# A recurrence with four experts behind it: three weight loads moved, four copies given to VectorE, VectorE's stated order changed

## The chip, the cores and the metric

The kernel runs on one core of one Trainium2 chip. A core has TensorE (PE) for matrix products, with a part of its own for loading the stationary operand (PEld in the profile), VectorE (DVE), ScalarE (ACT), GpSimd (POOL), and SyncE (SP), which here issues nearly all transfers (DMAs). Products land in PSUM, all else lives in SBUF. The metric is device time in microseconds (us), as the median of several runs; times inside an execution come from one profiled execution, counted from its first instruction.

## The reference

Two blocks follow each other, all in float32. The first is a recurrence over 768 tokens for 4 batches and 8 heads of width 40 (`[4, 8, 768, 40]` for each of r, k, v, w, a, b), with a state of 40x40 for each batch and head:

```python
for t in range(S):
    y[:, :, t] = np.einsum('bhd,bhde->bhe', rt, state)
    Sa = np.einsum('bhde,bhe->bhd', state, at)
    state_decay = state * wt[:, :, None, :] - np.einsum('bhd,bhe->bhde', Sa, bt)
    state = state_decay + np.einsum('bhd,bhe->bhde', vt, kt)
```

Its output becomes x of 3072 tokens by 320. The second block mixes four experts for each token:

```python
p = domain_probs / (domain_probs.sum(-1, keepdims=True) + 1e-09)
for e in range(E):                      # E = 4, F = 1024
    h = np.maximum(x @ w1[e], 0.0)
    out += p[:, e:e + 1] * (h @ w2[e])
```

## The kernel before

**Units and steps.** The tokens of a batch are cut into 12 chunks of 64. A unit is one chunk of two batches, so there are 24 units; unit u has chunk u // 2. For each unit, `within` does the work that needs no state: the running product of w (`G`, by two transposes and a scan on VectorE), its inverse (`gp`), the transposed operands A, V and R (`AT`, `VT`, `RT`), and the products between tokens of the chunk (`pfe` and `pe`, copied as `F` and `ET`; `pc`, copied as `VC`; `pev`, copied as `EV`). `substitute` solves the triangular system of the chunk: VectorE makes `M` from blocks of `F` (L599 to L615), and then a chain of small operations on `Z` runs on GpSimd (L620 to L639). `merge` makes `Qc`, `QTc` and `QT` of it. `step` is the part with the state: `prn` (state times A, and the turned state), `RH` = `prn` + `EV` on VectorE (L700), then ScalarE copies `SN`, then `psat`, `pxr`, `SX` (VectorE, L441), `pdy`, the new state (L773, L774) and the output `Y`, which transfers from SBUF to SBUF place as x transposed (`xT`, L793).

**Where V and R are turned.** For units 0 to 2 the natural V and R are turned by TensorE (`pVT`, `pRT`, L112) and ScalarE copies each out of PSUM in three copies: one of 128 rows, two of 64 rows that also swap halves (L472, L474). From unit 3 on VectorE turns them by itself from `rawV` and `rawR` (L282), which come in by 16 small transfers a unit (`load_raw`), placed in SP's queue by `later` and `begin_later`, three or six at a time between pieces of the experts' work.

**The experts.** w1 is read anew for each chunk in pieces: piece k holds half of the columns of one expert, 512 KB and two of 64 KB (L341), into one of two `w1p` buffers, or for some early pieces into a `sums` buffer. `used(n)` issues the next piece once piece n's products stand in the program; the transfer itself waits until TensorE is done with the buffer. `up_last` does 16 products of 64x64 with a piece (`ph`, small), `up_main` 16 of 128x128, and ScalarE writes relu of them as `hs` (L827). For chunks from the second on the down product of two units is done in seven block products instead of eight: VectorE adds weights (`sum_w`, L915) and halves of `hs` (`a`, named sum_a, L950), TensorE makes `p`, and VectorE adds `p` by the gate into the output tile (`osb`, named out, L842). Three PSUM buffers are shared by `ph` and `p` (tag "mm"), five by the recurrence (tag "big").

**What sets the order.** TensorE runs in the order in which the program is written, which mixes pieces of the experts' work (`mix`, `gap`) between the parts of the recurrence. VectorE's order is written out by hand in `VECTOR_ORDER` for what stands in it (units 1 to 7 and the additions up to out23); each name is tied behind the one before it at the end of the kernel. Later instructions of VectorE are placed by a scheduler. In it stand, for the change: `VC2.0 blocks2.0 blocks2.1 ET2.0 M2`; `G5.0 sum_w1 ... gll5 RH3.0 RH3.1`; `G6.0 ... gll6 sum_w5 RH4.0 RH4.1`. SP works its queue in program order where `keep_in_program_order` says so, as for every piece.

The loop over units, u = 1 to 23, runs steps 1 to 23; while step u runs, unit u + 1 is merged, unit u + 2 is solved, and the loads of unit u + 3 are issued. In the profile step 2 begins (`prn`) at 109.69 us, step 3 at 143.39, step 4 at 175.92, step 5 at 218.15 and step 6 at 249.63.

Of the kernel before, what the change touches and what calls it, by code (L numbers as in the profile page):

```python
# [9 lines left out]
ALU = mybir.AluOpType  # L10
ACTF = mybir.ActivationFunctionType
AX = mybir.AxisListType
BEHIND = mybir.DependencyInfo(mybir.DependencyClass.NoSync, mybir.DependencyReason.DATA)


VECTOR_ORDER = """
    Qc1 QTc1 G2.0 G2.1 gl2 G02 scan2 gll2 out1 gp2 1/gp2 N2 K2 AT2 AG2 VC2.0 blocks2.0 blocks2.1 ET2.0 M2 M02 Z12
    Z22 ET2.1 VC2.1 out2 G3.0 G3.1 gl3 G03 scan3 SX1.1 gll3 SX1.0 VT3 RT3 AT3 AG3 Y1.1 Y1.0 S+1.0 S+1.1 SG1.0 SG1.1
    gp3 1/gp3 N3 K3 out3 VC3.0 VC3.1 Qc2 QTc2 RH2.0 RH2.1 G4.0 G4.1 gl4 G04 blocks3.0 blocks3.1 M3 M03 Z13 Z23 ET3.0
    ET3.1 out4 scan4 gll4 AT4 AG4 SX2.0 SX2.1 VT4 RT4 Y2.1 Y2.0 S+2.0 YG2 SG2.0 S+2.1 gp4 SG2.1 1/gp4 N4 K4 out5  # L20
    VC4.1 VC4.0 sum_w0 Qc3 QTc3 ET4.0 blocks4.0 blocks4.1 ET4.1 M4 M04 Z14 Z24 G5.0 sum_w1 G5.1 gl5 G05 scan5 gll5
    RH3.0 RH3.1 sum_w2 AT5 AG5 out6 SX3.0 SX3.1 sum_w3 VT5 Y3.1 Y3.0 S+3.0 YG3 SG3.0 S+3.1 gp5 SG3.1 1/gp5 RT5 N5 K5
    sum_w4 out7 VC5.1 VC5.0 Qc4 QTc4 ET5.0 blocks5.0 blocks5.1 ET5.1 M5 M05 Z15 Z25 G6.0 G6.1 gl6 G06 scan6 sum_a4
    gll6 sum_w5 RH4.0 RH4.1 sum_w6 AT6 AG6 sum_a0 sum_a1 sum_a2 sum_a3 SX4.0 SX4.1 sum_w7 VT6 sum_w8 Y4.1 Y4.0 S+4.0
    YG4 SG4.0 S+4.1 gp6 SG4.1 1/gp6 RT6 N6 K6 out8 out9 out10 out11 sum_a5 VC6.1 VC6.0 Qc5 QTc5 ET6.0 blocks6.0
    blocks6.1 ET6.1 out12 out13 M6 M06 Z16 Z26 out14 out15 sum_w9 sum_a6 G7.0 G7.1 gl7 G07 RH5.0 RH5.1 scan7 gll7
    sum_a7 sum_a8 sum_a9 AT7 AG7 out16 out17 out18 out19 sum_w10 sum_w11 SX5.0 SX5.1 sum_w12 sum_w13 sum_w14 sum_a10
    sum_a11 out20 sum_a12 out21 sum_a13 VT7 out22 sum_a14 out23
"""


# [1 line left out]
def kernel(  # L33
# [38 lines left out]
    nc = tc.nc  # L72

    B, H, S, D = r.shape
# [12 lines left out]
    names, made, stated_order = VECTOR_ORDER.split(), {}, []  # L87
# [30 lines left out]
    def big(name):  # L118
# [6 lines left out]
        out=ident[:], in_=ident[:], pattern=[[1, P]], compare_op=ALU.is_equal, fill=0.0,  # L125
# [5 lines left out]
    for t, n, op in ((upf, L, ALU.is_gt), (diagf, Q, ALU.is_equal)):  # L131
        nc.vector.memset(t[:], 1.0)
        for q in range(P // n):
            o = slice(q * n, (q + 1) * n)
            nc.gpsimd.affine_select(
                out=t[o], in_=t[o], pattern=[[1, n]], compare_op=op, fill=0.0, base=0, channel_multiplier=-1,
# [153 lines left out]
    ins = nc.vector.transpose(out=unit_cols[:], in_=dealt(diagf[:, None, :].to_broadcast([P, H, Q])))  # L290
# [31 lines left out]
    def load_piece():  # L322

        k = len(pieces)
        e, x = k // 2 % E, k % 2
        if k in in_sums:
            t = sums[in_sums[k]]
        else:
            t = sb.tile([P, PIECE], FP32, name="w1p", tag="w1p", bufs=2)
        q = Piece()  # L330
        q.main = t[:, 0:2 * HF * P].rearrange("p (g c) -> p g c", g=2)
        q.last = t[:, 2 * HF * P:PIECE].rearrange("p (f c) -> p f c", c=P)
        cols = slice(x * HF * P, (x + 1) * HF * P)
        moves = [(q.main, moe_w1[e, 0:2 * P, cols].rearrange("(g p) c -> p g c", p=P))]
        for i in range(2):
            half_cols = slice((2 * x + i) * HF // 2 * P, (2 * x + i + 1) * HF // 2 * P)
            moves.append(
                (q.last[i * DT:(i + 1) * DT], moe_w1[e, 2 * P:DM, half_cols].rearrange("d (f c) -> d f c", c=P))
            )
        for to, src in moves:  # L340
            tc.keep_in_program_order(nc.sync.dma_start(out=to, in_=src))  # L341
        pieces.append(q)

    def used(n):
# [30 lines left out]
    def half(s):  # L375
        return slice(64 * s, 64 * s + 64)
# [66 lines left out]
    def within(q):  # L443

        n = q.n
# [12 lines left out]
        ins = nc.vector.tensor_tensor(out=q.gl[:], in0=G[:, L::L][:, :, None], in1=first[:, :, 0:1], op=ALU.mult)  # L458
# [4 lines left out]
        def turn_rv():  # L463
            VT = sb.tile([P, 2 * NJ, L], FP32, name="VT", tag="turned", bufs=3)
            q.RT = sb.tile([P, 2 * NJ, L], FP32, name="RT", tag="RT", bufs=2)
            for x, t in (("V", VT), ("R", q.RT)):
                if q.u >= PADDED:
                    noted(turn_raw(t[:], n["raw" + x][:]), x + "T", q.u)
                    continue
                p = turn(f"p{x}T", tok(n["padded" + x]), q.u == 1)[:].rearrange("p (j i t) -> p j i t", i=2, t=L)  # L470
                to = t[:].rearrange("p (i j) t -> p j i t", i=2)
                nc.scalar.copy(out=to[:, 0::2], in_=p[:, 0::2])  # L472
                for r in range(2):
                    nc.scalar.copy(out=to[half(r), 1::2], in_=p[half(1 - r), 1::2])  # L474
            return VT

        if q.u == 1:
# [66 lines left out]
        p = banks("pfe")  # L544
# [494 lines left out]
    def run(gen, n=99):  # L1039
        if gen is None:  # L1040
            return
        for _ in range(n):
            if next(gen, gen) is gen:
                break
# [111 lines left out]
    for u in range(1, NU):  # L1156
        in_order[0] = True
        q = units[u]
        m = s_next = w = w_next = iter(())
        if u + 1 < NU:  # L1160
            m, s_next = merge(units[u + 1]), begin_step(u + 1)
            w_next = ws[u + 1]
        if u + 2 < NU:
            w = ws[u + 2]

        def gap(n, pieces=None):
            here[0] = at = 4 * u + n
            run(sum_ops, sums_at.get(at, 0))
            mix((1 if at in sparse else 2) if pieces is None else pieces)

        early = u < EARLY
        if early:
            begin_later(len(later))
        ahead = u + 3 < NU and u in range(EARLY, EARLY + 3)
        if ahead:
            go(load_raw(begin(u + 3), "W"))
        if early:
            lead()
        if u == 1:
            run(s, 1)  # L1180
            run(w_next)
        else:
            run(w_next, 99 if early else 1)
            run(s, 1)
        gap(0)


        if early:
            run(s, 1)
        run(w, 1)  # L1190
        if not early:
            run(w_next)
            run(s)

        if early:
            run(w, 1)
            gap(1, 2 if u + 1 == EARLY else None)
            run(s)
        if u == 1:
            mixture_of_unit(q)  # L1200
        elif q.bp:
            mixture_of_chunk(units[u - 1:u + 1], chunks_x[q.c])
        if not early:
            begin_later(len(later))
            run(w, 1)
            lead()
            todo[:2] = todo[1::-1]
            gap(1)
            run(m, 1)

        if u + 3 < NU:
            if u == 1:
                go_now(load_raw(begin(4), "WVRA"))
            else:
                go(load_raw(units[u + 3] if ahead else begin(u + 3), "A" if ahead else "WA"))
            load(units[u + 3], "WBKV")
            if u > 1:
                later.extend(load_raw(units[u + 3], "VR"))
        run(w, 2)

        soon = u in (2, 3, 4)
        if soon:
            run(w, 1)
        if early:
            run(m, 1)
        else:
            run(m, 1)
            run(s_next, 1)
            lead()
            run(m, 1)  # L1230
            if u + 3 < NU:
                ws.append(within(units[u + 3]))
                run(ws[u + 3], 1)
        if soon:
            substitute(units[u + 2], nc.gpsimd)
        gap(2)

        if u == 1:
            run(s_next, 1)
            run(m, 1)  # L1240
        if not soon:
            run(w, 1)
        if not soon and u + 2 < NU:
            with sooner(not early):
                substitute(units[u + 2], nc.gpsimd)
        if not early:
            lead()
            run(s_next, 1)
        if early:
            run(w, 1)  # L1250
        if early:
            ws.append(within(units[u + 3]))
            run(ws[u + 3], 1)
            if u > 1:
                run(m, 1)
                run(s_next, 1)
            run(m)
            gap(3, 1)
            run(s_next, 1)
        else:  # L1260
            begin_later(len(later))
            gap(3)
        s = s_next
    mix(len(todo))
    for piece in last:
        piece()
    for one, then in zip(names, names[1:]):
        tc.add_manual_dep(made[then].ins, made[one].ins.name, BEHIND, reason="stated order of VectorE")


# [26 lines left out]
```

## Time and profile before

| | us |
|---|---|
| median of 3 runs | 1102.44 |
| lowest and highest of them | 1101.65, 1104.09 |
| the profiled execution | 1101.19 |
| its span, first to last instruction | 1099.5 |
| mean granted TensorE clock, share of full | 0.987 |

| engine | busy us | share of the span | instructions |
|---|---|---|---|
| TensorE products (PE) | 1071.3 | 97% | 16102 |
| TensorE loads (PEld) | 960.5 | 87% | 16102 |
| VectorE | 760.9 | 69% | 1551 |
| GpSimd | 491.5 | 45% | 1274 |
| ScalarE | 353.7 | 32% | 956 |

How to read what follows: a row of the timeline or of the chain of waits begins with start and length in us; a timeline row then has engine, line, operation, what is written and read, shapes, how many instructions were merged into it, and in brackets the idle time before it and what ended it. "issue" is time in which an engine waited for nothing that the profile names. A windows row begins with a stretch and its length, then has the busy time of each engine (instructions in brackets), the granted clock, the DMA share and GB/s. Product ends are modelled, since products are pipelined; a run of them is best timed from the first start to the next group's first start. Lines are those of the kernel before; line 109 and line 112 are the helpers through which every product and every turn goes, so products are told apart by their tiles.

### The profile page before, as it was taken

Reading aid. Unit: us, or ns where it says so; the run is one execution under the profiler, and the core shown is the slowest. Engines: PE = TensorE matmul, PEld = TensorE weight load, DVE = VectorE, ACT = ScalarE, POOL = GpSimd, SP = SyncE. Lnnn points to the kernel's source line nnn. Section 1 sums busy time; section 2 is a strip of 40 time slices with the busy share of each in tenths; the row PEclk is TensorE's granted clock in tenths of the full one; section 3 lists DMA queues with packets and bytes.
Section 4 is the critical chain, followed back from the end, with each engine's and each line's share of the span. In section 5 each row is a group of like instructions: output and inputs, shape, how many; then the busy total and the mean of one; then the engine's idle time right before and its main releaser. Section 6 shows DMA issues by size and latency. Waiting matters only on the chain.

```text
span 1099.5 us, 38531 instructions
## 1 busy us (share of the span) xinstructions
PE 1071.3 (97%) x16102; PEld 960.5 (87%) x16102; DVE 760.9 (69%) x1551; ACT 353.7 (32%) x956; POOL 491.5 (45%) x1274
## 2 busy tenths in 40 slices
PE   7899999999999999999999999999999999999998
PEld 6677777889988999999999989999999999988887
DVE  7676768788686767768668767767777686544343
ACT  2333444224233333233243243333333342321110
POOL 5206677573463653643734634625526527430000
PEclk8799999999999999999999999999999999999999
DMA  7876634334454364464453543444543532322320
GB/s 117 244 203 171 146 89 110 89 88 108 110 128 98 95 157 98 107 142 100 100 125 93 124 119 94 123 98 108 130 104 83 151 87 62 98 71 80 104 77 13
DMA packets 268869, 122.19 MB, mean 111 GB/s; under 512 B 213736, under 2 KB 242072, under 8 KB 268696
## 3 DMA queue, kind: packets, MB, share of 16 engines
q1 hardware_dynamic: 265416, 119.12, 44.1%
q8 instruction: 127, 2.08, 0.8%
q10 hardware_dynamic: 3280, 0.61, 0.3%
q14 instruction: 46, 0.38, 0.1%
HBM read 111.79 MB, written 3.93 MB: 105 GB/s over the span
## 4 chain that ended last, share of the span: by engine, by line
PE 88%; DVE 4%; ACT 2%; POOL 2%; issue 2%; DMA 1%; SPq 1%; ACTq 0%; DVEq 0%; POOLq 0%
PE ph L109 38%; PE p L109 31%; PE pdy L109 3%; PE psat L109 2%; PE pxr L109 2%; PE prn L109 2%; PE pfe L109 1%; PE pc L109 1%; PE pQ L109 1%; PE pg L112 1%; PE pev L109 1%; POOL Z L639 1%; DVE Z L636 1%; PE pe L109 1%; PE pY L109 1%
## 5 line engine op out<-in xcount | busy, mean ns | idle before, releaser
L109 PE MATMUL ph<-xT,w1p 128*128 128x256 f32 (+3 forms) x3040 | 446.0, 376 | 3.7 <-issue 3.5
L109 PEld LDWEIGHTS ph<-xT,w1p 64*64 64x64 f32 (+1 forms) x3040 | 338.9, 162 | 60.1 <-issue 17.7
L639 POOL TENSOR_TENSOR Z<-Z 128x31 f32<-128x31 f32 (+7 forms) x704 | 258.1, 367 | 55.2
L950 DVE TENSOR_TENSOR a<-hs 128x512 f32<-128x512 f32 x220 | 153.4, 715 | 111.6 <-ACT hs L827 111.6
L827 ACT ACTIVATE hs<-ph 128x512 f32<-128x512 f32 (+1 forms) x208 | 117.1, 564 | 329.3 <-PE ph L109 328.9
L626 POOL TENSOR_TENSOR Z<-M,Z 128x62 f32<-128x62 f32 (+7 forms) x352 | 145.4, 413 | 96.8 <-DVE M L615 71.0
L109 PE MATMUL p<-sums,a 128*128 128x160 f32 x1056 | 164.9, 299 | 0.0
L842 DVE SCALAR_TENSOR_TENSOR osb<-p,gate,osb 128x320 f32<-128x320 f32 (+1 forms) x243 | 108.0, 481 | 68.0 <-PE p L109 63.0
L109 PEld LDWEIGHTS p<-sums,a 128*128 128x128 f32 x1056 | 152.8, 190 | 2.2
L596 POOL COPY below<-F 32x256 f32<-32x256 f32 x48 | 22.5, 468 | 230.7 <-ACT F L551 229.1
L109 PEld LDWEIGHTS p<-w,hs 128*128 128x128 f32 x704 | 98.6, 190 | 8.5 <-issue 7.3
L109 PE MATMUL p<-w,hs 128*128 128x160 f32 x704 | 104.9, 302 | 0.0
L109 PE MATMUL p<-w,a 128*128 128x160 f32 x704 | 102.8, 299 | 0.0
L109 PEld LDWEIGHTS p<-w,a 128*128 128x128 f32 x704 | 98.0, 190 | 0.0
L657 POOL COPY QT<-QTc 32x256 f32<-32x256 f32 x96 | 40.4, 421 | 88.7 <-DVE QTc L651 77.6
L747 ACT COPY RS<-pxr 64x256 f32<-64x256 f32 x88 | 32.3, 367 | 102.7 <-DVE SX L441 68.0
L580 ACT COPY EV<-pev 64x160 f32<-64x160 f32 x96 | 23.0, 286 | 91.9 <-PE pev L109 91.5
L495 DVE RECIPROCAL gp<-gp 128x320 f32<-128x320 f32 x24 | 51.6, 2151 | 0.7
L441 DVE COPY_PREDICATED VC<-mask_up,pc 128x256 f32<-128x256 int32 x48 | 18.8, 442 | 47.5 <-PE pc L109 47.5
L599 DVE STREAM_TRANSPOSE M<-blocks 128x1024 f32<-128x1024 f32 x24 | 47.3, 1969 | 2.9 <-ACT blocks L592 2.7
L551 ACT COPY F<-pfe 128x256 f32<-128x256 f32 x48 | 15.5, 376 | 80.7 <-PE pfe L109 80.6
L109 PE MATMUL pdy<-VC,k_tok 64*64 64x104 f32 (+1 forms) x768 | 38.2, 259 | 0.0
(149 smaller groups left out, 1346.8 us busy)
## 6 DMA issues: line engine op xcount, KB each, us to landing
w1p<-in_moe_w_dram SPq DMA_DIRECT2D x95, 512.0 KB
w1p<-in_moe_w_dram SPq DMA_DIRECT2D x190, 64.0 KB
w<-in_moe_w_dram SPq DMA_DIRECT2D x4, 1280.0 KB
sums<-in_moe_w_dram SPq DMA_DIRECT2D x9, 512.0 KB
natW<-in_w_dram SPq DMA_DIRECT2D x48, 80.0 KB
natB<-in_b_dram SPq DMA_DIRECT2D x48, 80.0 KB
natK<-in_k_dram SPq DMA_DIRECT2D x48, 80.0 KB
out_dram<-osb SPq DMA_DIRECT2D x46, 80.0 KB
```

The lines of the kernel that those rows point to most:

```text
L109: return stated(nc.tensor.matmul(**k))
L495: pin(noted(nc.vector.reciprocal(out=gp[:], in_=gp[:]), "1/gp", q.u))
L580: nc.scalar.copy(out=of_slot(q.EV[half(p)], i ^ p)[:, :, 0:D], in_=pev[i][half(p)])
L596: tc.keep_in_program_order(nc.gpsimd.tensor_copy(out=q.below[quarter(i)], in_=q.F[quarter(i), :, 0:Q]))
L599: ins = nc.vector.transpose(out=M[:], in_=cols)
L626: ins = eng.tensor_tensor(out=Z[:, 1:3, 0:n, j + 1:Q], in0=M[:, j:j + 2, None, j + 1:Q].to_broadcast([P, 2, n, m]), in1=Z[:, here, 0:n, j: ...
L639: eng.tensor_tensor(out=z[:, 0], in0=z[:, 0], in1=z[:, x], op=ALU.add)
L657: ins = nc.gpsimd.tensor_copy(out=q.QT[quarter(i), :, quarter(i % 2)], in_=QTc[quarter(i)])
L747: nc.scalar.copy(out=RS[half(s), x ^ s::2], in_=prs[x][half(s)].rearrange("p (j i) t -> p j i t", i=2),)
L827: ins = nc.scalar.activation(out=h[:, i * HF // 2:(i + 1) * HF // 2, 0:n], in_=ph[i][:], func=ACTF.Relu,)
L842: ins = nc.vector.scalar_tensor_tensor(out=to, in0=p, scalar=sc, in1=to, op0=ALU.mult, op1=ALU.add)
L950: ins = nc.vector.tensor_tensor(out=t[:], in0=x, in1=y, op=op)
```

## The change

There are four edits.

1. The first transfer of every piece is given a name (`piece0`, `piece1`, ...), and at the end two of them are made to wait (a semaphore wait, `AFTER`) for a VectorE instruction: piece 13 for SX2.1, piece 22 for SX5.0. SP works in order, so all that stands behind in its queue waits too.
2. In the round u = 3, all loads of V and R that are left in `later` are issued before `gap(3, 1)`. In the built program the three transfers of piece 19 then stand behind two loads of V and eight of R, which were behind it.
3. For unit 2, one of the three copies of V (the second of 64 rows) and all three of R are done by VectorE. In VectorE's order they stand behind AG2; ET2.0 goes from before M2 to behind Z22.
4. In VectorE's order RH3 goes ahead of G5, RH4 ahead of G6. And two additions into the output, out45 and out61, go ahead of one sum each (sum_a27, sum_a37) and of the turns of A of units 9 and 10 (AT9, AT10).

```diff
+AFTER = mybir.DependencyInfo(mybir.DependencyClass.Sync, mybir.DependencyReason.DATA)
 BEHIND = mybir.DependencyInfo(mybir.DependencyClass.NoSync, mybir.DependencyReason.DATA)
...
-    ... AT2 AG2 VC2.0 blocks2.0 blocks2.1 ET2.0 M2 M02 Z12 Z22 ET2.1 VC2.1 out2 ...
-    ... M4 M04 Z14 Z24 G5.0 sum_w1 G5.1 gl5 G05 scan5 gll5 RH3.0 RH3.1 sum_w2 AT5 ...
-    ... M5 M05 Z15 Z25 G6.0 G6.1 gl6 G06 scan6 sum_a4 gll6 sum_w5 RH4.0 RH4.1 sum_w6 AT6 ...
+    ... AT2 AG2 VTc2.2 RTc2.0 RTc2.1 RTc2.2 VC2.0 blocks2.0 blocks2.1 M2 M02 Z12 Z22 ET2.0 ET2.1 VC2.1 out2 ...
+    ... M4 M04 Z14 Z24 RH3.0 RH3.1 G5.0 sum_w1 G5.1 gl5 G05 scan5 gll5 sum_w2 AT5 ...
+    ... M5 M05 Z15 Z25 RH4.0 RH4.1 G6.0 G6.1 gl6 G06 scan6 sum_a4 gll6 sum_w5 sum_w6 AT6 ...
...
-        for to, src in moves:
-            tc.keep_in_program_order(nc.sync.dma_start(out=to, in_=src))
+        for n, (to, src) in enumerate(moves):
+            ins = nc.sync.dma_start(out=to, in_=src)
+            tc.keep_in_program_order(ins)
+            if n == 0:
+                noted(ins, "piece")
...
-                nc.scalar.copy(out=to[:, 0::2], in_=p[:, 0::2])
-                for r in range(2):
-                    nc.scalar.copy(out=to[half(r), 1::2], in_=p[half(1 - r), 1::2])
+                places = [(to[:, 0::2], p[:, 0::2])]
+                places += [(to[half(r), 1::2], p[half(1 - r), 1::2]) for r in range(2)]
+                for at, (o, p_) in enumerate(places):
+                    if q.u == 2 and (x == "R" or at == 2):
+                        noted(nc.vector.tensor_copy(out=o, in_=p_), x + "Tc", q.u, at)
+                    else:
+                        nc.scalar.copy(out=o, in_=p_)
...
             run(m)
+            if u == 3:
+                begin_later(len(later))
             gap(3, 1)
...
-    for one, then in zip(names, names[1:]):
+    moved = [(out_, x) for out_, a_, u_ in ((45, 27, 9), (61, 37, 10)) for x in (f"sum_a{a_}", f"AT{u_}")]
+    for one, then in [*zip(names, names[1:]), *((f"out{n}", x) for n, x in moved)]:
         tc.add_manual_dep(made[then].ins, made[one].ins.name, BEHIND, reason="stated order of VectorE")
+    for k, then in ((13, "SX2.1"), (22, "SX5.0")):
+        tc.add_manual_dep(made[f"piece{k}"].ins, made[then].ins.name, AFTER, reason="weights not beside dense products")
```

More of the change, by code (lines that the diff above doesn't have):

```diff
@@ L12 @@
 AX = mybir.AxisListType
+AFTER = mybir.DependencyInfo(mybir.DependencyClass.Sync, mybir.DependencyReason.DATA)
 BEHIND = mybir.DependencyInfo(mybir.DependencyClass.NoSync, mybir.DependencyReason.DATA)
 VECTOR_ORDER = """
-    Qc1 QTc1 G2.0 G2.1 gl2 G02 scan2 gll2 out1 gp2 1/gp2 N2 K2 AT2 AG2 VC2.0 blocks2.0 blocks2.1 ET2.0 M2 M02 Z12
-    Z22 ET2.1 VC2.1 out2 G3.0 G3.1 gl3 G03 scan3 SX1.1 gll3 SX1.0 VT3 RT3 AT3 AG3 Y1.1 Y1.0 S+1.0 S+1.1 SG1.0 SG1.1
-    gp3 1/gp3 N3 K3 out3 VC3.0 VC3.1 Qc2 QTc2 RH2.0 RH2.1 G4.0 G4.1 gl4 G04 blocks3.0 blocks3.1 M3 M03 Z13 Z23 ET3.0
@@ L20 @@
[L20 to L28, printed above, removed]
+    Qc1 QTc1 G2.0 G2.1 gl2 G02 scan2 gll2 out1 gp2 1/gp2 N2 K2 AT2 AG2 VTc2.2 RTc2.0 RTc2.1 RTc2.2 VC2.0 blocks2.0
@@ new lines @@
+    blocks2.1 M2 M02 Z12 Z22 ET2.0 ET2.1 VC2.1 out2 G3.0 G3.1 gl3 G03 scan3 SX1.1 gll3 SX1.0 VT3 RT3 AT3 AG3 Y1.1
+    Y1.0 S+1.0 S+1.1 SG1.0 SG1.1 gp3 1/gp3 N3 K3 out3 VC3.0 VC3.1 Qc2 QTc2 RH2.0 RH2.1 G4.0 G4.1 gl4 G04 blocks3.0
+    blocks3.1 M3 M03 Z13 Z23 ET3.0 ET3.1 out4 scan4 gll4 AT4 AG4 SX2.0 SX2.1 VT4 RT4 Y2.1 Y2.0 S+2.0 YG2 SG2.0 S+2.1
+    gp4 SG2.1 1/gp4 N4 K4 out5 VC4.1 VC4.0 sum_w0 Qc3 QTc3 ET4.0 blocks4.0 blocks4.1 ET4.1 M4 M04 Z14 Z24 RH3.0
+    RH3.1 G5.0 sum_w1 G5.1 gl5 G05 scan5 gll5 sum_w2 AT5 AG5 out6 SX3.0 SX3.1 sum_w3 VT5 Y3.1 Y3.0 S+3.0 YG3 SG3.0
@@ new lines @@
+    S+3.1 gp5 SG3.1 1/gp5 RT5 N5 K5 sum_w4 out7 VC5.1 VC5.0 Qc4 QTc4 ET5.0 blocks5.0 blocks5.1 ET5.1 M5 M05 Z15 Z25
+    RH4.0 RH4.1 G6.0 G6.1 gl6 G06 scan6 sum_a4 gll6 sum_w5 sum_w6 AT6 AG6 sum_a0 sum_a1 sum_a2 sum_a3 SX4.0 SX4.1
+    sum_w7 VT6 sum_w8 Y4.1 Y4.0 S+4.0 YG4 SG4.0 S+4.1 gp6 SG4.1 1/gp6 RT6 N6 K6 out8 out9 out10 out11 sum_a5 VC6.1
+    VC6.0 Qc5 QTc5 ET6.0 blocks6.0 blocks6.1 ET6.1 out12 out13 M6 M06 Z16 Z26 out14 out15 sum_w9 sum_a6 G7.0 G7.1
+    gl7 G07 RH5.0 RH5.1 scan7 gll7 sum_a7 sum_a8 sum_a9 AT7 AG7 out16 out17 out18 out19 sum_w10 sum_w11 SX5.0 SX5.1
@@ L29 @@
+    sum_w12 sum_w13 sum_w14 sum_a10 sum_a11 out20 sum_a12 out21 sum_a13 VT7 out22 sum_a14 out23
 """
```

## The prediction

> **What bounds the kernel now.** I read the page first, then the list of waits of TensorE, then the chain of waits, then narrow windows around each hole in the chain.
>
> ```profile
> PE 1071.3 (97%) x16102; PEld 960.5 (87%) x16102; DVE 760.9 (69%) x1551; ACT 353.7 (32%) x956; POOL 491.5 (45%) x1274
> ...
> q8 instruction: 127, 2.08, 0.8%
> ```
>
> TensorE is busy 97% of the span of 1099.5 us, so the change can gain only what TensorE loses to holes (28 us, some eleven of them before the first step of the recurrence) and to slow stretches. Above 360 us the same group of work comes back every 42.4 to 42.7 us with almost no hole; everything to be won lies before that. Queue q8 brings instructions: 2.08 MB over 127 packets of 16 KB, for 32,204 TensorE instructions, is one packet for some 254 instructions.
>
> ```profile
> PE ph L109 <- issue: 4.0, 5, 1.3
> PE pxr L109 <- issue: 2.5, 1, 2.5
> PE pc L109 <- ACT RT L472: 1.5, 2, 0.8
> ```
>
> Of these the first two rows wait for nothing that the profile names. The chain of waits shows the longest in its place, in step 4 of the recurrence (start, length, what):
>
> ```profile
> 185.44 0.50 PE pxr L109 x26
> 185.94 2.51 issue
> 188.46 1.33 PE pxr L109 x35
> 189.78 6.12 PE ph L109 x16
> ...
> 330.73 3.45 PE ph L109 x16
> ```
>
> The reader is to see two losses: the hole of 2.51, and behind it 16 products in 6.12 where the same 16 take 3.45 elsewhere. The windows say why (columns: stretch, length, PE, PEld, DVE, ACT, POOL, granted clock, DMA share, GB/s):
>
> ```profile
> 182.40:185.90 3.50, 3.50 (x142) 3.20 (x142) 3.08 (x5) 3.34 (x11) 3.03 (x7) 1.00 0.51 169
> 185.90:188.40 2.50, 0.04 (x2) 0.00 (x0) 1.18 (x2) 0.89 (x4) 2.19 (x5) 0.90 0.37 82
> 188.40:194.80 6.40, 6.34 (x47) 5.24 (x47) 2.89 (x5) 2.06 (x5) 5.46 (x13) 0.50 0.17 32
> ```
>
> Before the hole TensorE ran 284 instructions in 3.5 us (64x64 products), more than one packet of them; after it the granted clock was 0.50 for 6.4 us. The DMA view of 176 to 185.9 us has no packet on q8; extended to 187.1 us it has one:
>
> ```profile
> q8 instruction: 1, 0.02, 0.6%
> ```
>
> In the trace that packet starts at 186.00, takes 1.00, and TensorE goes on 1.46 later. SP had issued piece 19 (512 KB) at 182.59; its 2048-byte packets fill 183.5 to 186. So the instruction packet stood behind the weights. The same picture stands at 228.06 (piece 22 issued at 223.67, instruction packet 227.06 to 228.04, hole 1.30, no drop of the clock) and, short, at 123.0 (hole 0.50).
>
> Two other kinds of hole: VectorE, in its stated order, stands before something late.
>
> ```profile
> 150.75 0.29 PE L109 MATMUL psat<-QT,RH 64*64 64x64 f32 x2 [0.73 <-ACT QT L673]
> ...
> 302.25 0.71 DVE L282 STREAM_TRANSPOSE AT<-rawA 128x512 f32<-128x512 f32 x1 [1.75 <-DMA rawA<-in_a_dram]
> 302.89 0.51 DVE L842 SCALAR_TENSOR_TENSOR osb<-p,gate,osb 128x320 f32<-128x320 f32 x1
> ...
> 304.39 0.87 PE L109 MATMUL ph<-xT,w1p 64*64 64x256 f32 x11 [0.47 <-issue]
> ```
>
> **The change part by part.** In the built programs TensorE's and GpSimd's streams are the same; only VectorE's, ScalarE's and SP's move. All times are of the profiled execution (1101.19 us, span 1099.5).
>
> *Unit 2's VT and RT (ACT to DVE).* ScalarE does six copies of 0.37 to 0.39 from 81.59 to 83.90; `pc` waits 0.73 and 0.42 for them and `po` starts at 84.46. Four go to VectorE, which is idle for 8.36 us there. No row has this copy on VectorE; bounds are 0.27 (blocks copy) and 0.44 (predicated copy out of PSUM). I take 0.44, nearest because it reads PSUM: pVT and pRT are written by 80.7 and 81.2, so four end by 82.5, when `pfe` ends too (82.45). `pc` takes 0.52 elsewhere, so `po` starts at 83.05: -1.4. The M transpose of unit 2 starts 0.44 earlier besides, since an ET copy goes behind it; GpSimd's Z chain (M to Qc, 20 us) then ends 1.8 earlier, and the 0.61 that `pY` waits at 111.47 shrinks by 0.4. Against it, ET2.0 now ends at 88.1, when `pxr` and `pev` want its bank and data: up to +0.5. Sum -1.8, bounds -0.7 and -2.0.
>
> *RH3 and RH4 ahead of G and scan.* RH3 runs at 149.78 behind two transposes, gl, a scan of 1.22 and a sum, though its products ended at 144.44. ScalarE's SN and QT stand behind RH3, psat behind QT. Moved up, RH3 ends at 147.1 and QT at 148.6, before `po` ends (149.8). Psat starts at 149.95 instead of 150.75, and takes 0.95 as in other steps instead of 1.90: -1.7 (-0.8, the start alone, to -1.75). Next late are SX3, at 153.3, with pxr. RH4 likewise: psat 1.34 to 0.95 and its late start: -0.45 (0 to -0.8). G and scan come 0.55 later; their users (pg, AT) lie 15 us on or follow in the same queue. Of the Z chain: GpSimd waits 2.5 before QT4, of which 1.27 is always there, and `pY` of that step comes 3.5 after QTc, so it does not become the bound.
>
> *Piece 19 behind ten loads.* SP issues V's last two and R's eight loads (0.47 each, 4.7 us) first, then piece 19 near 186.3 instead of 182.59. Used at 201.42; its data took 4.4 us from issue, so it has 10 us left. The instruction packet, wanted at about 182.8 (the count of instructions since the last one), now meets small packets: one wanted at 143.97, with R loads under way, started 1.00 later. So: 183.9 start, 1.00, 1.4 to use: 186.3, against 185.65 where TensorE runs out. A hole of 0.7 stays; I expect no clock drop, as at the hole of 1.30. Gain: 2.51 + (16 and 34 products at half clock, 6.3 us, half of it 3.1) - 0.7 = -4.9. Bounds: -5.6 (no hole) and -2 (the hole drops the clock again).
>
> *Piece 22 behind SX5.0.* Issue 223.67 to 228.6. `ph` x32 takes 6.51 there and 4.58 in the next units: 1.93; a rest of 0.3 stays: -1.6 (-0.6 to -1.9). Behind it on SP stand V and R loads, four W loads and piece 23, each 4.9 later; SP is idle from 237.87 to 243.91, which takes it up. VectorE's VT at 237.83 needs the V loads, landing near 235.7: 2 us left; RT at 247.83 and piece 23 (used at 250.61) have more.
>
> *Piece 13 behind SX2.1.* 119.88 to 123.4. Its hole of 0.50 mostly stays covered: `ph` at 124.99 waits for ScalarE's hs, behind RS, behind SX2. -0.1 (0 to -0.6). Forty transfers behind it shift 3.5; SP then idles 8.5 us (148.78 to 157.24).
>
> *out45 and out61 ahead of a sum and A's turn.* AT9 waits 1.75 and AT10 4.41 for rawA, and the sums that free PSUM for `ph` stand behind. `ph` (13) and psat take 1.73 and 2.54 where 0.87 is usual. With the sums first AT finds its data landed: -0.8 and -1.6 (at least a third of each, if `ph` is held by something else too; at most 0.85 and 1.67).
>
> [...]
>
> New small waits in the early units (DMA and GpSimd chains that don't shorten): +0.4. Sum: -1.8 -1.7 -0.45 -4.9 -1.6 -0.1 -0.8 -1.6 +0.4 = **-12.5**. The profiled execution would go to 1088.7; it lies 1.25 under the median of the three runs, so the median goes from 1102.4 to **1089.9**.
>
> **Rivals.** *(a) The instruction packet stays late* behind the small loads at 185.9, and the clock drops again: piece 19 gives -2, piece 22 -0.6: -8.6, 1093.8; with the lower bounds of the others -4.5, 1097.9. For: a packet wanted at 168.5 beside loads of natB and natK started 2.2 late. Against: 1.00 beside R loads. *(b) The pieces were not the cause* (the change doesn't do what it says): VectorE's and ScalarE's parts alone stay, -1.8 -1.7 -0.45 -0.8 -1.6 +0.4 = -6.0, 1096.4. Against: the trace's packet times. *(c) Slower: SP's queue.* Place: behind piece 22 at 228.6. If SP isn't caught up when Y's moves are due at 243.91, those come late, then piece 24, and TensorE stops long enough to lose its clock: 5.6 each time. It decides from about 6 us of delay; my 4.9 is near. Three such stops, 16.8, give 1106.7. Against: SP's idle 6.0 us there and the same again in each later unit.
>
> **How the numbers follow.** Forecast 0.62 (own range 1087 to 1092.5), (a) 0.17, (b) 0.08, (c) and other new stalls 0.10, gains and stalls cancelling 0.03. Faster is forecast, (a) and (b): 0.87; a measurement can't tell less than 0.2% (2.2 us) from none. All best bounds give some -15.2 or 1087.2; with 0.7 us for the spread of the runs the low end is 1086.5. The high end takes in (a) and (b): 1098; (c) is left out.
>
> **What would show it.** Step by step: `po` at about 83 with no wait of `pc`; psat of step 3 without its wait; no row "PE pxr <- issue" over 1 us and clock 1.00 from 184 to 196; `ph` x32 near 227 in under 5 us; AT9 and AT10 behind the sums, `ph` near 300 and 340 unbroken. After 360 us the period stays 42.5. Wrong would be: half clock near 185 to 195 again, SP's Y moves late, or VectorE waiting longer for V.

## The result and the profile after

On one chip the changed kernel took **1090.2 us** (median of 6 runs, 1089.31 to 1091.46) and the kernel before 1101.37 us (median of 6, 1096.56 to 1104.09): ratio 0.990, 95% interval 0.988 to 0.992. The forecast was 1089.9. The profiled execution took 1089.31 us with a span of 1087.6, 11.9 us under the span of before.

The page's first part, one line (busy time, share of the span, instructions):

```profile
PE 1063.5 (98%) x16102; PEld 955.6 (88%) x16102; DVE 762.5 (70%) x1555; ACT 352.0 (32%) x952; POOL 493.4 (45%) x1274
```

TensorE is busy 7.8 us less for the same 16102 products: the slow stretch is gone. The list of TensorE's waits (in total, times, longest) has lost its row "PE pxr <- issue", and shows new ones:

```profile
PE pc L110 <- DVE RT L480: 1.3, 2, 1.0
...
PE ph L110 <- ACT hs L835: 0.7, 1, 0.7
...
PE ph L110 <- issue: 0.3, 1, 0.3
```

The chain of waits from 180 to 206 us (start, length, what) covers the place of the old hole and a new loss:

```profile
180.68 1.07 PE psat L110 x64
181.75 0.89 PE ph L110 x16
...
183.08 1.03 PE pxr L110 x60
184.11 3.65 PE ph L110 x16
187.76 1.74 PE pdy L110 x61
...
205.00 0.57 PE ph L110 x2
205.57 0.28 issue
205.85 0.40 PE ph L110
```

The 64 products of `pxr` now run without the hole of 2.51, and the 16 of `ph` behind them take 3.65 in place of 6.12. The window over them (stretch, length, PE, PEld, DVE, ACT, POOL, granted clock, DMA share, GB/s) has the clock at full speed:

```profile
182.30:190.70 8.40, 8.40 (x194) 7.45 (x187) 7.54 (x14) 5.14 (x16) 7.44 (x13) 1.00 0.51 115
```

Where the 11.9 us came from, read by the start of the same product of TensorE in both traces (minus is gained in the changed kernel):

| from, to | change, us | what |
|---|---|---|
| start to `pdy` of step 2 | 0.0 | unit 2's copies, piece 13 |
| to `pdy` of step 3 | -1.75 | RH3 |
| to `pxr` of step 4 | -0.5 | RH4 |
| to `pdy` of step 4 | -5.86 | hole and half clock gone |
| to psat of step 5 | +0.92 | `ph` near 205, new |
| to `pdy` of step 5 | -1.95 | piece 22 |
| to `prn` of step 7 | +0.1 | small waits |
| to `pxr` of step 7 | -1.1 | out45, AT9 |
| to `pxr` of step 8 | -1.75 | out61, AT10 |
| the rest, 750 us | 0.0 | the steady part |

The table sets one execution against one, and the kernel before doesn't lose the same at each place every time. From `pxr` to `pdy` of step 4 it took 10.66 us here, and 9.52 and 8.71 us in two kernels below that change nothing up to there (out45 and out61 alone, piece 22 alone), against 4.80 in the changed kernel. A gain in the table is the size for this pair of executions, not a fixed price.

### The profile page after: what moved, and what is told of

The parts are those of the page before. It is cut to its first block, busy times and chain, and to the rows that moved or that the text cites. A ratio compares the mean times of both kernels' runs of the same rounds, so it can differ in the third digit from the quotient of the medians.

```text
span 1087.6 us, 38532 instructions
## 1 busy us (share of the span) xinstructions
PE 1063.5 (98%) x16102; PEld 955.6 (88%) x16102; DVE 762.5 (70%) x1555; ACT 352.0 (32%) x952; POOL 493.4 (45%) x1274
## 4 chain that ended last, share of the span: by engine, by line
PE 88%; DVE 4%; DMA 3%; ACT 2%; POOL 2%; SPq 1%; issue 1%; DVEq 0%; POOLq 0%; ACTq 0%
PE ph L110 38%; PE p L110 31%; PE pdy L110 3%; PE psat L110 2%; PE pxr L110 2%; PE prn L110 2%; DMA sums<-in_moe_w_dram 1%; PE pfe L110 1%; PE pc L110 1%; PE po L110 1%; POOL Z L647 1%; PE pQ L110 1%; PE pev L110 1%; PE pe L110 1%; PE pY L110 1%
## 5 line engine op out<-in xcount | busy, mean ns | idle before, releaser
L647 POOL TENSOR_TENSOR Z<-Z 128x31 f32<-128x31 f32 (+7 forms) x704 | 263.4, 374 | 55.2
```

The costliest lines, as they stand in the source:

```text
L647: eng.tensor_tensor(out=z[:, 0], in0=z[:, 0], in1=z[:, x], op=ALU.add)
```

## The experiments

The runs below come from three chips. The kernel before took 1098.2 us on that of the single parts (26 runs, 1094.1 to 1100.9), 1097.3 on that of the parts undone (7 runs) and 1096.2 on the last (one run), 3 to 5 us less than above. The changed kernel itself was not run beside them. Part of the spread is in the first 50 us: half clock held for 13.65 us in the shortest case and 27.31 us in the longest, and everything behind stood -1.7 to +1.6 us from the kernel before's profiled execution. So beside the times the text gives the gain between two products of one trace, which that start doesn't touch.

### One part alone, on the kernel before

**Piece 19.**

```diff
             run(m)
+            if u == 3:
+                begin_later(len(later))
             gap(3, 1)
```

> The kernel before with one edit: piece 19 behind the ten loads of V and R. Theory (the instruction packet stood behind the weights, and the hole dropped the clock): the row "PE pxr <- issue" of 2.5 us goes, the granted clock stays 1.00 from 184 to 196 us, and the time falls by 5.9 us, what the span between pxr and pdy of that step lost in the changed kernel, to about 1095.3 in a profiled execution. The new wait of 0.9 us that the changed kernel shows ahead of ph near 205 does not come, since TensorE's lead over GpSimd is smaller than the 6.6 us by which Qc followed GpSimd's last product in the kernel before. Rival (the piece was not the cause; what shortened the step was the earlier end of RH): the hole and the half clock stay, time within 0.5 us of before.

Measured: 1094.67 us, ratio 0.9971 (0.9957 to 0.9984). Windows before, in and behind the hole:

```profile
183.90:187.20 3.30, 3.30 (x140) 3.10 (x142) 2.88 (x5) 3.17 (x10) 2.91 (x6) 1.00 0.28 54
187.20:188.40 1.20, 0.27 (x17) 0.13 (x10) 1.20 (x2) 1.06 (x5) 1.04 (x3) 1.00 0.13 22
188.40:194.50 6.10, 6.10 (x116) 5.21 (x115) 3.13 (x6) 2.66 (x6) 5.24 (x12) 1.00 0.52 143
```

The clock stays 1.00, but a hole of 0.93 remains, and from `pxr` to `pdy` of step 4 the gain is 4.6 us, not 5.9. The packet, with piece 19 out of its way, still started only at 185.60, behind `psat`'s start at 184.01. So the weights are a cause, and not the whole one. No wait came where the changed kernel has one near 205, as expected.

**Piece 22.**

```diff
+    for k, then in ((22, "SX5.0"),):
+        tc.add_manual_dep(made[f"piece{k}"].ins, made[then].ins.name, AFTER, ...)
```

> The kernel before with one edit: piece 22 behind SX5.0. Theory: the hole of 1.30 us near 228 goes, the 32 products of ph there take 4.6 us in place of 6.5, gain 1.9 us, to about 1099.2. Rival one (piece not the cause): no change. Rival two (SP's queue pays for the wait): V's turn near 238 or Y's moves come late, and the gain is under 1 us or below nothing.

Measured: 1096.26 us, ratio 0.9984 (0.9969 to 1.0), which reaches no change. The chain of waits there, in the kernel before and with piece 22 held:

```profile
227.20 0.87 PE ph L109 x12
228.06 1.30 issue
229.36 4.30 PE ph L109 x20
```

```profile
225.85 4.92 PE ph L110 x32
```

The 32 products take 4.92 in one piece, and 1.55 us are gained from `pxr` to `pdy` of step 5; no wait for V's loads or for Y's moves is new there. The packet there started at 223.81, ahead of `pxr` at 224.69; in the kernel before it was 227.06 with `pxr` at 226.04. The first theory holds in the trace, with 1.55 us for its 1.9.

**RH3 and RH4.**

```diff
-    ... Z14 Z24 G5.0 sum_w1 G5.1 gl5 G05 scan5 gll5 RH3.0 RH3.1 sum_w2 ...
+    ... Z14 Z24 RH3.0 RH3.1 G5.0 sum_w1 G5.1 gl5 G05 scan5 gll5 sum_w2 ...
-    ... Z25 G6.0 G6.1 gl6 G06 scan6 sum_a4 gll6 sum_w5 RH4.0 RH4.1 sum_w6 ...
+    ... Z25 RH4.0 RH4.1 G6.0 G6.1 gl6 G06 scan6 sum_a4 gll6 sum_w5 sum_w6 ...
```

> The kernel before with one edit: RH3 and RH4 ahead of G and the scan in VectorE's order. Theory (VectorE's order held psat): psat of step 3 loses its wait of 0.73 and takes 0.95 us, with step 4 together a gain of 2.2 us, to about 1099.0. But the hole at 185.9 stays. Rival (TensorE would wait for SX3 in its place): gain 0.8 or less.

Measured: 1092.15 us, ratio 0.9945 (0.9926 to 0.9964): some 6 us, not 2.2. The 1.75 us of step 3 are there, and then 5.86 us more from `pxr` to `pdy` of step 4: **the hole is gone though piece 19 was issued in its old place**, at 182.29. The packet started at 180.65, before the piece. No theory had said so, and it asks whether piece 19's move was worth anything in the changed kernel.

**out45 and out61.**

```diff
+    moved = [(out_, x) for out_, a_, u_ in ((45, 27, 9), (61, 37, 10)) for x in (f"sum_a{a_}", f"AT{u_}")]
```

> The kernel before with one edit: out45 and out61 ahead of a sum and A's turn. Theory (the sums that free PSUM stood behind A's data): AT9 and AT10 find their data landed, gain 1.1 and 1.75 us, together 2.85, to about 1098.3. Rival (ph is held by something else too): a third of that, 0.95.

Measured: 1096.2 us, ratio 0.9986 (0.9972 to 0.9999). In the trace 1.10 us come between `prn` and `pxr` of step 7, and 1.75 between those of step 8, the numbers of the changed kernel, and A's turn of unit 9 has no wait left:

```profile
L282 DVE STREAM_TRANSPOSE AT<-rawA 128x512 f32<-128x512 f32 x1 | 0.7, 704 | 0.0
```

The theory holds, but not the 2.85 us as a fixed size: against the kernels with this edit, the seven other kernels without it lose 0.14 to 1.47 us at the first place and 0.41 to 1.26 at the second. The medians give 2.0 us. The profiled execution lost 0.9 again between 803 and 823 us, in a part that the edit doesn't touch.

### One part undone, on the changed kernel

**Piece 19 back in its place.**

```diff
-            if u == 3:
-                begin_later(len(later))
```

> The changed kernel with one part undone: piece 19 ahead of the last two loads of V and the eight of R, as before. Theory one (the weights block the instruction packet wherever they stand; the gains of the parts add): the hole of 2.5 us and the half clock come back, 5.9 us more than the changed kernel, some 1096. Theory two (with RH3 and RH4 early TensorE asks for that packet near 178, ahead of piece 19's issue near 181, as the run with RH alone showed: start 0.9 us after, no hole): no hole, time within 0.5 us of the changed kernel, and piece 19's move adds nothing in this company.

Measured: 1089.76 us against 1097.32 of before, ratio 0.992 (0.9902 to 0.9937). From the 70th to the 455th us every product is 1.1 to 1.2 us later than in the changed kernel, a shift that came with the start (half clock for 23.89 us where the changed kernel had 20.48). Over the old hole and behind it:

```profile
181.70:183.50 1.80, 1.80 (x81) 1.56 (x84) 1.76 (x4) 1.17 (x4) 1.57 (x4) 1.00 0.25 71
183.50:191.80 8.30, 8.30 (x194) 7.34 (x187) 7.45 (x14) 5.09 (x16) 7.36 (x13) 1.00 0.50 130
```

No hole, clock 1.00. Theory two holds in the trace, which takes 4.81 us from `pxr` to `pdy` of step 4 where the changed kernel takes 4.80: beside the early RH, piece 19's move adds nothing there. The medians can't be set against each other, since the two were not run side by side.

**Unit 2's copies.**

```diff
-                    if q.u == 2 and (x == "R" or at == 2):
+                    if False:
```

with ET2.0 back ahead of M2 in VectorE's order.

> The changed kernel with one part undone: unit 2's VT and RT copied by ScalarE alone, ET2.0 ahead of M2. Theory (these copies brought nothing, since VectorE's first of them waited until 82.42 for ScalarE's second and the four then ran one behind the other to 84.18): po at 84.5 in place of 84.7, time within 0.3 us of the changed kernel. Rival (the term of the prediction holds, but was given back later): 1.5 us slower.

Measured: 1088.2 us, ratio 0.9912 (0.9891 to 0.9933). `pc` of unit 2 starts 0.73 earlier than in the changed kernel, 0.48 of it from the start of the run, and by `pY` of step 2 nothing else is left. Up to there the copies brought nothing. (Further on, near 167, this execution loses 0.35, with a wait of 0.21 for VectorE's `n_tok`; all three traces with RH3 early and these copies on ScalarE have that wait, and none of the four with copies on VectorE. Then this execution doesn't lose the 0.92 near 205, since Qc waits 0.76 there and not 1.82.)

**R's copies alone.**

```diff
-                    if q.u == 2 and (x == "R" or at == 2):
+                    if q.u == 2 and x == "R":
```

with VTc2.2 out of VectorE's order.

> The changed kernel with VT's third copy back on ScalarE, so that VectorE has RT's three alone and waits for none of ScalarE's. Theory (the order held VectorE's copies, not their duration): RT's copies run from 81.2 to 82.5, VT's on ScalarE end at 82.8, pc starts at 82.85 and po at 83.4, 1.3 us ahead of the changed kernel, and M2 as much earlier, so that the time falls by 1.3 us or by as much as pY of that step doesn't wait for GpSimd. Rival (VectorE's copies start late whatever their order, or GpSimd's chain takes it all back): within 0.3 us.

Measured: 1086.92 us, ratio 0.9898 (0.9881 to 0.9915). VectorE's and TensorE's groups there, in the changed kernel:

```profile
L110 PE MATMUL pc<-RT,VT 40*64 40x64 f32 x32 | 1.0, 228 | 1.3 <-DVE RT L480 1.3
...
L480 DVE COPY VT<-pVT 64x256 f32<-64x256 f32 x1 | 0.4, 419 | 6.2 <-ACT VT L482 6.2
```

and with R's copies alone:

```profile
L110 PE MATMUL pc<-RT,VT 40*64 40x64 f32 x32 | 1.0, 225 | 0.3 <-ACT VT L482 0.3
...
L480 DVE COPY RT<-pRT 128x256 f32<-128x256 f32 x1 | 0.4, 425 | 5.0 <-PE pRT L113 5.0
```

The last column says what VectorE's first copy waited for: ScalarE's second copy of the same tile VT in the one, the products themselves in the other. `pY` of step 2 comes 1.28 us earlier than in the changed kernel, net of the start. The theory holds: one copy at the head of the row held the other three.

**R's copies alone, and out12 and out13 moved up.**

```diff
-    VC6.0 Qc5 QTc5 ET6.0 blocks6.0 blocks6.1 ET6.1 out12 out13 M6 ...
+    VC6.0 Qc5 QTc5 out12 out13 ET6.0 blocks6.0 blocks6.1 ET6.1 M6 ...
```

> The kernel with RT's copies alone on VectorE, and out12 and out13 moved from behind ET6.1 to behind QTc5. Theory (the 0.9 us lost in the changed kernel near 205 are TensorE's ph waiting for the PSUM that these two sums free, and they stand behind Qc5, which waits 1.82 for GpSimd): the 32 products of ph there take 4.7 in place of 5.6 us; with the 1.3 of unit 2, 2.2 us less than the changed kernel, near 1088. Rival (ph waits for something else): 1.3 less, ph keeps 5.6.

Groups near 200 to 206 us in the changed kernel:

```profile
L110 PE MATMUL ph<-xT,w1p 64*64 64x256 f32 x6 | 1.1, 414 | 0.3 <-issue 0.3
...
L658 DVE STREAM_TRANSPOSE Qc<-Z 128x256 f32<-128x256 f32 x1 | 0.6, 630 | 1.8 <-POOL Z L647 1.8
L850 DVE SCALAR_TENSOR_TENSOR osb<-p,gate,osb 128x320 f32<-128x320 f32 x1 | 0.5, 545 | 0.0
```

and in this one:

```profile
L110 PE MATMUL ph<-xT,w1p 64*64 64x256 f32 x12 | 0.9, 393 | 0.0
...
L658 DVE STREAM_TRANSPOSE Qc<-Z 128x256 f32<-128x256 f32 x1 | 0.6, 628 | 1.4 <-POOL Z L647 1.4
```

Qc waits for GpSimd in both, but the two sums end at 203.35 in place of 205.75, ahead of `ph`, and the 32 products take 4.67 in place of 5.59: 0.92 us less than in the changed kernel, as the theory has it. The size is not fixed: with R's copies alone the 32 took 5.18, and with all of unit 2's copies on ScalarE 4.67 too, both with out12 and out13 in their old place. Measured time: 1088.26 us, ratio 0.9909 (0.9891 to 0.9927). Net of the start this trace is 1.7 us ahead of the changed kernel (a hole of 0.37 at 90 us took some back) and the one before it 1.5 us; the medians can't tell these versions from the changed kernel.

### What holds the packet

Four variants of the kernel before, one execution each, ask why the early RH did what it did.

**R's loads held, with piece 19 ahead of them and then behind them.**

```diff
     def begin_later(n):
...
+            noted(ins, "late")
...
+    tc.add_manual_dep(made["late24"].ins, made["SX4.0"].ins.name, AFTER, reason="held")
```

The second has the edit of piece 19 besides.

> The kernel before with R's eight loads of unit 6 held behind SX4.0; piece 19 and two loads of V stay where they were. Theory one (the packet stands behind the weights' bytes): it starts when piece 19's data end, 185.5 to 186, the hole stays at 2 us or more. Theory two (the small loads hold the packet as well, since with piece 19 behind them it still came 3.6 us late): without R's loads it starts a microsecond or more earlier, near 184.5, and the hole is 1.3 or less. In both RT and piece 20 come later; what that costs shows after 195 us and doesn't bear on the hole.

Measured: start of the packet 184.79, `psat` at 182.07, hole 1.69, clock 1.00 behind it. That lies between the theories: 2.72 us behind `psat` where the kernel before has 3.50.

> The kernel before with R's eight loads and piece 19, in this order, held behind SX4.0, so that SP issues nothing between the last load of V and SX4.0. Both theories: with no transfer in its way the packet starts about 1 us after its request near 181, as where SP is idle elsewhere, no hole, clock 1.00, and pdy of that step 5.9 us earlier against pxr than in the kernel before. If the packet comes late all the same, transfers are not what holds it. Piece 19 lands near 198, some 2 us after ph wants it: a wait there of 2 to 3 us is the price of this edit, not part of the question.

Measured: hole 0.83, against both theories. SP issued its last load of V by 182.8, and V's last data packet started before 184.0. The DMA view from 178 us to 184.2, and to 185.6, shows when the instruction packet came:

```profile
q1 hardware_dynamic: 1651, 0.88, 49.8%
```

```profile
q1 hardware_dynamic: 1651, 0.88, 40.7%
q8 instruction: 1, 0.02, 1.1%
```

It started at 184.25, 1.4 us behind `psat` (182.88), with nothing but the last small loads of V ahead of it. Loads of V are under way in all these kernels, in the one with the early RH too, whose packet started 1.35 us ahead of `psat`. So transfers alone don't hold it; it seems **asked for late**. The wait for piece 19 cost 1.4 us near 198.

**RH3 alone, RH4 alone.** The edits are the two halves of the diff above.

> The kernel before with RH3 alone ahead of G and the scan. If the earlier request of the packet is what saved the step in the run with RH3 and RH4: RH3's 1.7 us come ahead of that request (near 180), so the packet starts within 1.5 us of it, no hole, clock 1.00: 1.7 and 5.9 us, together 7.6 from psat of step 3 to pdy of step 4. Rival (that run was luck): the hole of 2 us or more stays, gain 1.7.

> The kernel before with RH4 alone ahead of G and the scan. The request of the packet comes ahead of RH4's effect, so the hole of 2 to 2.7 us stays, and the granted clock falls behind it for one or two stretches of 3.4 us; gain in psat of step 4 about 0.4. Rival (that run was luck, or any shift will do): no hole.

Measured, the other way round: with RH3 alone the hole stays (1.48 us, packet at 183.38), with RH4 alone it is gone (packet at 179.27, 5.86 us gained from `pxr` to `pdy` of step 4, for the execution of before in the table). The DMA view of RH4 alone from 176 to 180.7 us, just short of its `psat` at 180.75, already has the packet:

```profile
q8 instruction: 1, 0.02, 1.4%
```

That of RH3 alone has none up to 183.3, though its `psat` starts at 180.43. My reading of the run with both, that RH3's lead had moved the request, fell. RH3 alone doesn't keep its gain either: of the 1.75 us some 0.8 are left at `pxr` of step 4, mostly since `psat` there waits longer for QT. Groups from 174 to 186 us, RH3 alone:

```profile
L109 PE MATMUL psat<-QT,RH 64*64 64x64 f32 x32 | 1.5, 228 | 0.3 <-ACT QT L673 0.2
...
L109 PE MATMUL pxr<-RT,SaT 64*64 64x64 f32 x31 | 1.0, 226 | 1.5 <-issue 1.5
...
L706 ACT COPY SN<-prn 128x256 f32<-128x256 f32 x2 | 0.7, 367 | 4.7 <-DVE RH L700 4.7
```

RH4 alone:

```profile
L109 PE MATMUL pxr<-RT,SaT 64*64 64x64 f32 x32 | 0.8, 225 | 0.0
...
L706 ACT COPY SN<-prn 128x256 f32<-128x256 f32 x2 | 0.7, 365 | 0.2 <-DVE RH L700 0.2
...
L109 PE MATMUL psat<-QT,RH 64*64 64x64 f32 x32 | 0.7, 224 | 0.0
```

With RH4 late, ScalarE's SN and QT stand behind it, and QT's copies end in the very moment in which TensorE comes to `psat` of step 4 and has to wait for them. With RH4 early the last of them ends 2.4 to 3.1 us ahead of `psat`. This sorts all fourteen kernels (us; start of the packet counted from `psat` of step 4):

| kernel | QT's last copy, from `psat` | packet, from `psat` | hole |
|---|---|---|---|
| before; out45 and out61 alone | +0.4 | +3.5 | 2.5; 2.7 |
| piece 22 alone; RH3 alone | +0.4; +1.0 | +2.9 | 1.9; 1.5 |
| R held | +0.4 | +2.7 | 1.7 |
| piece 19 alone | +0.4 | +1.6 | 0.9 |
| R and piece 19 held | +0.4 | +1.4 | 0.8 |
| changed; RH3 and RH4; RH4 alone; the four with one part of the changed kernel undone or moved | -2.4 to -3.1 | -0.9 to -1.6 | none |

The first five rows have RH4 late, the last has it early. Two things add up: where `psat` has to wait, the packet doesn't start before `psat` does, and comes 1.4 us behind it with the last loads of V alone under way, 1.6 with loads of V and R, 2.7 to 3.5 with piece 19 too. Where `psat` finds its data, the packet starts 0.9 to 1.6 us ahead of it, and then piece 19 is too late to be in its way.

Counted in TensorE's products and loads, the places are the same in every trace. All seven kernels with a hole stop 282 instructions behind `psat`'s first, as they would if the next packet is what they lack there. In the seven without one the packet starts while TensorE is 6 to 12 instructions ahead of `psat`'s first; in the others it is 135 to 282 behind.

The trace doesn't record the request itself; that TensorE's stream reads ahead, up to the instruction that waits, is my reading of these starts, and no run here shows it directly.

## Why the prediction was right, and where it wasn't

The sum was right to 0.6 us (-11.9 for -12.5), by terms of which one failed, one was laid to the wrong edit, and one new loss was not named. That they cancel is luck: unit 2's 1.8 and the new loss were made up by terms that came out larger than worked out. So it is with the median: 1090.2 for 1089.9 holds a gain of 11.2 for 12.5 and a kernel before that took 1.1 us less in six runs than in the three that the forecast started from.

- **Unit 2's copies: -1.8, measured 0.** The step that failed is "pVT and pRT are written by 80.7 and 81.2, so four end by 82.5". The duration was right (0.42 for 0.44). But the first of the four is VT's third, which waited until 82.42 for ScalarE's second copy of the same tile, and the three of R stood behind it: they ended at 84.18, and `pc` waited for them instead. R's three alone gained 1.28. Undoing the copies cost only some 0.4 us near 167, which the prediction did not name.
- **RH3: -1.7, measured -1.75.** Right in place and size; without RH4 it gives back more than half by `pxr` of step 4.
- **RH4: -0.45, measured -0.5 of its own (0.43 with RH4 alone), and with it the 5.86 of the hole.** The prediction moved QT ahead of `psat` and counted only `psat`'s own time. It had no line for what else comes late behind a waiting instruction on TensorE: the next packet, and, as its starts tell it, the asking for it.
- **Piece 19: -4.9, measured -5.86 at this place, though not by this edit.** Its working was right for the kernel before: wanted at about 182.8, 1.00 behind that beside small loads, "a hole of 0.7 stays", no clock drop. Piece 19 alone did that: wanted behind 184.01, started 1.6 later, hole 0.93, gain 4.6. What failed is "wanted at about 182.8" as a fixed time: with RH4 early the packet starts 0.9 to 1.6 us ahead of `psat`, ahead of the piece, and undoing piece 19's move costs nothing. That the loss passed the bound of 5.6 is the half clock, worked out over 6.3 us and granted for 6.83. Either edit takes most of this loss, and the two don't add.
- **Piece 22: -1.6, measured -1.95** (1.55 alone). Right in mechanism, slightly over the bound of 1.9; seven other kernels without the edit lose 1.05 to 1.82 there. SP's queue took up the shift, and rival (c) did not come.
- **Piece 13: -0.1, measured 0.** The hole of 0.50 went and `ph` waits 0.67 for ScalarE's hs instead, as worked out. The 0.50 was a good case: with piece 19 alone this place held a hole of 1.98, and `pdy` of step 2 came 1.0 later; step 3, which waits for the late RH3, took that up.
- **out45, out61: -0.8 and -1.6, measured -1.1 and -1.75.** Right mechanism, both slightly over the bounds that I gave as the most (0.85 and 1.67), in this execution of before; other traces lose less at the second place, and less or more at the first.
- **New small waits: +0.4, measured about +1.0**, nearly all of it one wait. The prediction said of GpSimd's chain that "it does not become the bound". That held for the gain of 2.2 us that it had in mind; after 5.9 us more it did: the chain took 25.7 us (24.6 before), Qc, which had followed its end by 6.6 us, waited 1.82 for it, and the sums behind Qc kept `ph` from its PSUM. Nor is this loss fixed: of the other kernels with RH4 early and out12 in its old place, one loses 0.92 there too, one 0.5, and three 0.15 or nothing. Where several gains come ahead of one chain, its slack has to be set against their sum.

Of the rivals, (a), the packet late behind the small loads, came in part with piece 19 alone (1.6 us behind `psat`), without its clock drop; (b), that the pieces were not the cause, is refuted for 22 and half true for 19.

## What to carry to other kernels

A wait on TensorE can cost more than its own length, as the 0.4 us that `psat` of step 4 waited for QT did (RH4 alone took 5.86 us behind it away), when the next instruction packet comes late with it: ahead of a dense stretch, look not only at what TensorE waits for but at when the next instruction packet starts, and whether a large transfer gets in between. When two edits can take the same loss, only runs with one of them undone tell which did; a sum that fits shows neither. And a copy that goes to an idle engine stands there in a row (unit 2's first waited until 82.42 us and the last of the four ended at 84.18; R's three alone gained 1.28): put the one that waits for another engine last.

## What the runs showed that I had not expected

- An instruction packet can come late with only small loads in its way, and the runs point to the instruction ahead of it that waits: 1.4 us behind `psat` with R's loads and piece 19 held, and 1.35 ahead of it, with piece 19 in its old place, where `psat` didn't wait.
- The clock fell in or just behind holes of 2.75, 2.51 and 1.92 us (out45 and out61 alone, the kernel before, piece 22 alone), for 3.41, 6.83 and 3.41 us, and not with holes of 1.98 and 1.69; so in these runs the hole's length alone doesn't decide it.
- At the kernel's start the half clock held for 13.65 to 27.31 us in different executions, and carried up to 3.3 us between the earliest and the latest of them through to the end.
